# A DeltaNet and feed-forward kernel: the early Gram products, outputs, weight combinations and dummy matmuls are re-ordered

## The chip, the core and the metric

The kernel runs on one core of a Trainium2 chip. The metric is the device time of one execution in microseconds (us). Engines are named as in the profile: PE (TensorE, matmuls), PEld (its weight loads), DVE (VectorE), ACT (ScalarE), POOL (GpSimd) and SP (SyncE, which here only issues DMAs). ACT and POOL issue some DMAs as well.

## What is computed

The first part is a delta-rule attention over 4 batches, 8 heads, 768 steps and a head size of 48. The second is a feed-forward layer over the 3072 rows that come out of it.

```python
k_n = k / (np.linalg.norm(k, axis=-1, keepdims=True) + 1e-06)
for t in range(S):
    y[:, :, t] = np.einsum('bhd,bhde->bhe', q[:, :, t], state)
    v_old = np.einsum('bhde,bhd->bhe', state, kt)
    state = state + bt[:, :, :, None] * np.einsum('bhd,bhe->bhde', kt, vt - v_old)
...
x = y.transpose(0, 2, 1, 3).reshape(B * S, H * D)      # 3072 x 384
h = x @ w_in                                           # 384 x 2048
g = h * (1.0 / (1.0 + np.exp(-1.702 * h)))
return g @ w_out                                       # 2048 x 384
```

The weights arrive as 64-bit floats, so the kernel itself turns the raw words into 32-bit floats.

## The kernel before, in words

**Units.** The 768 steps are cut in 6 chunks of 128. A unit is one chunk of one batch, with all 8 heads; unit n is chunk n // 4 of batch n % 4, and there are 24. A unit needs: its keys scaled to length one; `turn(n)` (line 435), the keys transposed by PE through PSUM into kT; `gram(n)` (412), the product of the keys with themselves per head, copied from two PSUM tiles into G by two copies; `send_blocks` (461), which writes the four 32 x 32 diagonal blocks per head to DRAM (four DMAs, `Nd<-G`); `load_diagonals` (471), which reads them back as one row per block into NT; `invert` (476), which inverts the triangular blocks on DVE (rows `P`, `YB`, `NT`), writes them out (`Yd<-NT`) and reads them back as XB. Then come scores (QS, M), and the solve in four blocks of 32 rows: `solve` (psU) multiplies the inverse with V and ACT copies the result to US, `below` (psR) multiplies it with G, and DVE subtracts that from the rows of V below (`rest`). `outputs` (700) forms psY and the state (psS, added to ST by DVE), ACT copies to xT, and after every second unit six small DMAs move rows of `last` into xT.

**Start.** Chunk 0 (units 0 to 3) has its grams and inversion first. Units 4 to 7 follow: their squares and roots are taken together, and `roots_second` (384) scales the keys of 4 and 5 by 16 ACT copies and those of 6 and 7 by two DVE products. Then the four units of chunk 0 are solved in two pairs. `hops(a, b)` (1090) yields, for a pair, the eight sets of solves and belows, in which one unit's solve shares the set with the other's below; `together` (929) issues a set. Between sets, `fill(us)` (304) issues about so many us of DVE work from a background queue: first the conversion of w_in in nine pieces (`conversions`, 259; each piece is four DVE steps with one ACT Relu and a fifth DVE step), then invert(1) for units 4 to 7, then the conversion of w_out. `feed` (1125) issues six matmuls of the feed-forward layer's first product (`hidden`, 729; PSUM tile ph).

**Steady part.** From line 1170 on, `woven` (975) interleaves the chain of one unit with the matmuls of the feed-forward layer, which `spend` (966) takes from a queue. `normalize` (316) scales the keys of unit m = n + 5 in three stages: POOL squares and DVE sums them; POOL takes the root (`rn`, L325); DVE adds and inverts and POOL multiplies the keys (L329). The rows of the feed-forward layer are multiplied two tiles of 128 at a time with seven half-size products instead of eight (`seven`, 786). For that, `combined` (771) makes T1 to T4 from quarters of w_out in 16 subtractions on POOL (line 762), T1, T2 and T4 into three slots of the buffer TW, T3 in place. TW also holds, at other times, keys of unit 7 and 11 (KX, words 3072 to 3583), the queries, and the GELU results of units 2 and 3.

**Order.** What is called through `vec`, `act`, `pe`, `pool`, `sync` (SP) or `beside` (ACT's DMA queue) is kept in program order on its engine or queue by the helper at line 108, so most rows of the profile name L108, and tiles tell them apart. What is called through `nc.gpsimd` or `nc.sync` directly (normalize, masks and L762 among them) is placed by the compiler's own plan. `warm(n)` (137) issues n dummy bf16 matmuls of 128 x 256 into a PSUM tile that nobody reads.

Of the kernel before, what the change touches and what calls it, by code (L numbers as in the profile page):

```python
# [18 lines left out]
def kernel(  # L19
# [32 lines left out]
    HB = 2  # L52
# [84 lines left out]
    def warm(n, after=None):  # L137
        ps = ps_moe.tile([128, 256], F32, tag="moe", name="ps_warm")
        if after is not None:
            after(ps[:, 0:1], 0.0)  # L140
        for _ in range(n):
            pe.matmul(ps, lhsT=ones[:, 0:128], rhs=ones, start=True, stop=True)
# [66 lines left out]
    def conversion(dst, raw, shape):  # L209

        lo, hi = raw[:, :, :, 0], raw[:, :, :, 1]
        ts, stt = vec.tensor_scalar, vec.scalar_tensor_tensor
        AND, OR = ALU.bitwise_and, ALU.bitwise_or
        E1 = 1 << 20
        p = dst.bitcast(I32)
        ts(p, hi, 0x7FF * E1, None, op0=AND)  # L220
        act.activation(p, p, ACT.Relu, scale=8.0, bias=low)
        yield 0.75
        stt(out=p, in0=hi, scalar=-(1 << 31), in1=p, op0=AND, op1=OR)
        yield 0.95
        ts(hi, hi, E1 - 1, E1, op0=AND, op1=OR)
        yield 0.7
        f = lo.bitcast(F32)
        stt(out=f, in0=lo.bitcast(U32), scalar=2.0**-32, in1=hi, op0=ALU.mult, op1=ALU.add)
        yield 0.95
        stt(out=dst, in0=f, scalar=2.0**-20, in1=dst, op0=ALU.mult, op1=ALU.mult)  # L230
        yield 0.95
# [27 lines left out]
    def conversions():  # L259

        whole = list(pieces())

        def begin(i):
            dst, raw, shape, name = whole[i]
            ops = conversion(dst, places[name[1]] if raw is None else raw, shape)
            return ops, next(ops)

        after, cost = begin(0)
        yield cost
        for i in range(len(whole)):  # L270
            ops = after
            yield next(ops)
            yield next(ops)
            if i + 1 < len(whole):
                after, cost = begin(i + 1)
                yield cost
            yield next(ops)
            cost = next(ops)
            done.add(whole[i][3])
            fetches.pop(whole[i][3], lambda: None)()  # L280
            yield cost
# [31 lines left out]
    def home(n):  # L313
        return KX if n in (len(KN), 3 * B - 1) else KN[n % len(KN)]
# [69 lines left out]
    def roots_second(areas):  # L384

        z, r = (TW[:, a : a + B * H].rearrange("p (b h) -> p b h", b=B) for a in (1792, 1856))
        for o in range(2):
            vec.tensor_reduce(z[:, 2 * o : 2 * o + 2], areas[o], axis=AX.X, op=ALU.add)
        pool.tensor_tensor(r, z, half[:, 0:1].broadcast_to([128, B, H]), op=ALU.pow)
        yield  # L390
        vec.tensor_scalar(r, r, 1e-6, None, op0=ALU.add)
        vec.reciprocal(r, r)
        for o in range(HB):
            K = home(B + o)[:, :, 0:D]
            for h in range(H):
                act.activation(K[:, h], K[:, h], ACT.Copy, scale=r[:, o, h : h + 1])
        yield
        for o in range(HB, B):
            K = home(B + o)[:, :, 0:D]
            vec.tensor_tensor(K, K, r[:, o].broadcast_to([128, H, D]), op=ALU.mult)  # L400
        gate = wk.tile([128, 1], F32, tag="gate", name="gate", bufs=1)
        pool.tensor_copy(gate, KX[:, 0, 0:1])
        yield

    def transposed(src, dst):
        psT = ps_big.tile([128, NP, 128], F32, tag="big", name="psT")
# [5 lines left out]
    def gram(n):  # L412

        c, b = units[n]
        kT = kTs[n]
        G = wk.tile([128, H, 128], F32, tag="G", name="G", bufs=6)
        pool_, tag = (ps_seq, "seq") if c == 0 else (ps_big, "big")
        ps = [pool_.tile([128, NP, 128], F32, tag=tag, name="psG") for _ in range(2)]
        for h in range(H):
            r = slice(h % 2 * 64, h % 2 * 64 + D)  # L420
            pe.matmul(
                ps[h % 2][:, h // 2], lhsT=kT[r, h // 2, :], rhs=kT[r, h // 2, :],
                start=True, stop=True,
            )
        act.activation(G[:, 0::2], ps[0], ACT.Copy)
        if B <= n < 2 * B + HB:
            act.activation(G[:, 1::2], ps[1], ACT.Copy)
        else:
            vec.tensor_copy(G[:, 1::2], ps[1])
        ready[n] = KN[n % len(KN)], kT, G  # L430
        return G

# [43 lines left out]
    def invert(c, b0=0, nb=B):  # L476
# [62 lines left out]
            )  # L539
            yield 0.35 + Q * HS * n / 480  # L540
        if c == 0:
            warm(NY, vec.memset)
        YS = N
        vec.tensor_tensor(YS, Y, bc, op=ALU.mult)
        if c == 0:
# [24 lines left out]
    class Step:  # L570
# [129 lines left out]
        def outputs(self, state=False, between=None):  # L700
            self.turned(
                (0, 4, 1, 5, 2, 6, 3, 7),
                lambda h: self.US[:, h * D : h * D + DP], lambda h: self.M[:, h, :],
                self.c == 0,
            )
            if state:
                self.state(self.psS, between)
            t = slice(self.b % HB * C, (self.b % HB + 1) * C)
            if t.start == 0:
                lasts[0] = wk.tile([128, NTH], F32, tag="last", name="last", bufs=1)  # L710
            last = lasts[0]
            act.copy(last[:, t], self.psY[1][:, 1, :])
            act.copy(self.xT[:, 0::2, t], self.psY[0])
            act.copy(self.xT[:, 1, t], self.psY[1][:, 0, :])

            if t.start > 0:
                t, dma = slice(0, NTH), sync if self.c == 0 else nc.sync.dma_start
                for ct in range(2):
                    for j in range(KC):
                        dma(  # L720
                            out=self.xT[ct * DP + D : (ct + 1) * DP, j, t],
                            in_=last[ct * DP + j * XR : ct * DP + (j + 1) * XR, t],
                        )
# [37 lines left out]
    def add(o, a, b, op, engine=None):  # L761
# [2 lines left out]
    W11, W21 = w_out[:, 0:HF, 0:HM], w_out[:, HF:, 0:HM]  # L764
    W12, W22 = w_out[:, 0:HF, HM:], w_out[:, HF:, HM:]
    T1, T2, T4 = (
        TW[:, i * HF * HM : (i + 1) * HF * HM].rearrange("p (f d) -> p f d", f=HF) for i in range(3)
    )
    T3 = W12

    def combined():

        n = 2
        for o, a, b in ((T1, W12, W11), (T2, W22, T1), (T3, W22, W12), (T4, W21, T2)):
            for f in range(0, HF, n):
                add(o[:, f : f + n], a[:, f : f + n], b[:, f : f + n], sub_)
                yield

    def beside_of(work, other):

        for cost in work:
            next(other, None)
            yield cost
        run(other)

# [118 lines left out]
    def run(work):  # L904
        for _ in work:
            pass
# [38 lines left out]
    def follow(n):  # L945

        if n + 3 < len(units):
            load(n + 3, ((QP, q),))
        m = n - 1 + len(KN)
        if n == B + 1:  # L950
            nc.sync.dma_start(out=KN[m % len(KN)], in_=KX)
        elif n > B and m < len(units):
            load(m, ((KN, k),), nc.gpsimd.dma_start)
        if n - 1 + B < len(units):
            load_values(n - 1 + B)
        if n % HB == 0 and n > B:
            h = (n - 1) // HB
            gT, sums = [], []
            work = hidden(xTs[h], gT, slice(0, NTH), 1.3, sums)
            queue.append(beside_of(work, combined()) if h == HB else work)  # L960
            queue.append(seven(*units[h * HB], gT, sums))
            xTs.pop(h)

    debt = [0.0]

    def spend(cost):

        debt[0] = debt[0] + cost if queue else 0.0
        for done in take(debt[0]):
            debt[0] -= done  # L970
# [4 lines left out]
    def woven(n, share):  # L975
# [24 lines left out]
        ahead_of(inverting, ahead[1])  # L1000
        spend(share / 6)
        next(P, None)
        spend(share / 6)

        together([(B_, 2)], [(D_, 0)])
# [74 lines left out]
        turn(n)  # L1080
    for n in (B, B + 1):
        gram(n)
    run(inverting)
    Ndx = [send_blocks(n) for n in (B, B + 1)]
    run(scaling)
    pool.memset(late_U[:, H * D :], 0.0)
    for s in pair:
        s.select()

    def hops(a, b):  # L1090

# [8 lines left out]
        s.outputs(True, lambda: fill(1.7))  # L1100
        steps.pop(s.n)

    path = hops(*pair[:2])
    for i in range(2 * NB):
        together(*next(path))
        if i in (1, 3):
            turn(B + HB + i // 2)
        if i > 0:
            fill(1.7)
    for n in (B + 2, B + 3):  # L1110
        gram(n)
        Ndx.append(send_blocks(n))
    load_diagonals(Ndx)
    for s in pair[:2]:
        put_out(s)
    sync(out=KN[0], in_=KX)
    load(8, ((KN, k),), sync)
    for f in range(3):
        fetch_out(f)
    for n in range(B, B + 2):  # L1120
        load(n, ((QP, q),), sync)
# [7 lines left out]

    gTs = [], []  # L1130
    ffn.append(hidden(xTs[0], gTs[0], slice(0, NTH), 1.3))
    path = hops(*pair[2:])
    for i in range(2 * NB):
        together(*next(path))
        if i > 2:
            feed()
        fill(1.7)
    for s in pair[2:]:
# [80 lines left out]
```

## Time and profile before

| what | value |
|---|---|
| median of 3 runs | 778.43 us (774.37 to 779.09) |
| profiled execution | 778.5 us, its span 776.8 us |
| PE busy | 730.6 us (94%), 8356 matmuls |
| DVE busy | 487.7 us (63%) |
| ACT busy | 238.6 us (31%) |
| POOL busy | 237.7 us (31%) |
| mean granted PE clock | 0.947 |
| 28 dummies of chunk 0's inversion | 61.37 to 66.79 us |
| first hop of units 0 and 1 | 66.7 us |
| grams of units 6 and 7 on PE | 85.2 to 90.5 us |
| invert(1) starts on DVE | 114.6 us |

A row of a timeline reads: start in us, duration in us, engine, line, operation, out<-in, shapes and count, and in square brackets the idle time of the engine just before and what ended it. A row of the table by stage reads: from and to, then for PE, PEld, DVE, ACT and POOL the busy time and in brackets the number of instructions, then the granted PE clock (1.00 is full, 0.50 is half), the share of the DMA engines and GB/s. A busy PE includes matmuls that are slow for a lower clock.

### The profile page before, as it was taken

The numbers are of one execution on the slowest core, as the hardware profiler recorded it, in microseconds if no ns is written. First come the engines' busy times: TensorE is split into PE (matmuls) and PEld (weight loads), VectorE is DVE, ScalarE is ACT, GpSimd is POOL, SyncE is SP. The second block draws the span as 40 slices with busy tenths as digits, with TensorE's granted clock in tenths as the row PEclk, the third lists the DMA queues.
The fourth block names the chain that finished last, engine by engine and source line by source line (L and its number), as shares of the span: only waits on it lengthen the run. The fifth ranks groups of instructions, "written<-read, shape, count | busy, mean of one in ns | idle before, by whom it ended". The sixth has DMA issues, their size and how long they took to land.

```text
span 776.8 us, 19495 instructions
## 1 busy us (share of the span) xinstructions
PE 730.6 (94%) x8356; PEld 626.8 (81%) x8356; DVE 487.7 (63%) x1013; ACT 238.6 (31%) x527; POOL 237.7 (31%) x210
## 2 busy tenths in 40 slices
PE   8388789989997999999999999999999999999998
PEld 6266668856666898898898898888988988988988
DVE  4796689999768577687687687677677750120000
ACT  3363443533332322422323322322322313222120
POOL 5022001200057362352442542542620611403123
PEclk8576679999999899999999999999999999999999
DMA  9994654531224104104113113113113020000000
GB/s 169 123 173 100 169 127 82 123 102 50 59 46 84 35 13 95 38 19 92 35 25 84 35 27 84 35 31 79 36 23 77 20 56 2 2 27 1 26 1 21
DMA packets 128182, 47.11 MB, mean 61 GB/s; under 512 B 117920, under 2 KB 122144, under 8 KB 128096
## 3 DMA queue, kind: packets, MB, share of 16 engines
q1 hardware_dynamic: 125568, 41.54, 25.7%
q0 software_dynamic: 1344, 3.93, 2.2%
q8 instruction: 66, 1.08, 0.6%
q10 hardware_dynamic: 1184, 0.39, 0.2%
q14 instruction: 20, 0.16, 0.1%
HBM read 33.13 MB, written 11.01 MB: 57 GB/s over the span
## 4 chain that ended last, share of the span: by engine, by line
PE 74%; DVE 15%; DMA 4%; issue 3%; SPq 2%; POOL 2%; ACT 1%; DVEq 0%; POOLq 0%; ACTq 0%
PE ph L108 28%; PE po L108 25%; PE psY L108 5%; PE psU L108 5%; DVE P L108 4%; PE psG L108 4%; PE psQ L108 3%; DVE YB L108 3%; DVE w_out L108 2%; SPq L108 2%; PE psT L108 2%; PE psR L108 2%; DVE NT L108 2%; DMA w_out<-in_moe_w_in_dram 1%; DMA Nd<-G 1%
## 5 line engine op out<-in xcount | busy, mean ns | idle before, releaser
L108 PE MATMUL ph<-xT,w_in 128*128 128x256 f32 x1152 | 266.7, 387 | 0.4 <-DMA xT<-last 0.4
L108 PEld LDWEIGHTS ph<-xT,w_in 128*128 128x128 f32 x1152 | 217.6, 193 | 33.1 <-DVE V L108 1.4
L108 PE MATMUL po<-w_out,gT 128*128 128x192 f32 (+1 forms) x736 | 147.2, 354 | 4.0 <-DVE o L108 3.6
L762 POOL TENSOR_TENSOR gT<-gT 128x512 f32<-128x512 f32 x80 | 105.9, 1332 | 123.9 <-ACT gT L108 113.4
L108 DVE TENSOR_TENSOR V<-V,psR 64x384 f32<-64x384 f32 (+1 forms) x96 | 53.3, 556 | 135.5 <-PE psR L108 134.2
L108 PEld LDWEIGHTS po<-w_out,gT 128*128 128x128 f32 x736 | 121.2, 191 | 19.6 <-DVE o L108 4.6
L108 ACT ACTIVATE gT<-ph 128x512 f32<-128x512 f32 x92 | 54.9, 596 | 147.0 <-PE ph L108 146.9
L108 DVE TENSOR_TENSOR P<-NT,YB 64x2 f32<-64x2 f32 (+9 forms) x200 | 96.0, 480 | 6.2
L108 PEld LDWEIGHTS psU<-V,XB 32*32 32x32 f32 x1536 | 61.3, 109 | 33.6 <-issue 12.8
L108 DVE TENSOR_REDUCE YB<-P 64x2 f32<-64x2 f32 (+9 forms) x200 | 81.8, 409 | 6.9
L108 PE MATMUL po<-TW,gT 128*128 128x192 f32 x480 | 83.0, 328 | 0.0
L108 ACT COPY US<-psU 32x384 f32<-32x384 f32 x92 | 43.2, 469 | 128.5 <-PE psR L108 117.5
L108 PE MATMUL psU<-V,XB 32*32 32x48 f32 x1536 | 72.4, 208 | 9.4 <-DVE V L108 9.2
L108 PEld LDWEIGHTS po<-TW,gT 128*128 128x128 f32 x480 | 77.9, 190 | 1.1 <-issue 0.3
L108 PE MATMUL psR<-US,G 32*32 32x48 f32 x2208 | 63.7, 207 | 4.2 <-ACT US L108 4.1
L108 DVE TENSOR_TENSOR o<-o,po 128x192 f32<-128x192 f32 x40 | 13.5, 351 | 75.8 <-PE po L108 75.3
L108 PEld LDWEIGHTS psR<-US,G 32*32 32x32 f32 x2208 | 54.0, 108 | 5.6 <-ACT US L108 4.9
L631 POOL TENSOR_SCALAR_AFFINE_SELECT M<-M 128x1024 f32<-128x1024 f32 x19 | 22.3, 1173 | 94.3 <-DVE M L108 62.4
L108 DVE TENSOR_TENSOR P<-NT 64x512 f32<-64x512 f32 (+7 forms) x50 | 44.1, 883 | 2.4 <-DVE NT L108 0.5
L108 PE MATMUL psG<-kT 48*128 48x128 f32 x384 | 36.3, 335 | 1.3 <-ACT G L108 1.0
L93 POOL DMA_DIRECT2D KN<-in_k_dram x12 | 11.5, 958 | 84.1 <-PE psY L108 84.1
L108 PE MATMUL psQ<-QS,kT 48*128 48x176 f32 (+1 forms) x368 | 34.5, 330 | 0.8 <-ACT QS L108 0.8
(118 smaller groups left out, 735.7 us busy)
## 6 DMA issues: line engine op xcount, KB each, us to landing
V<-in_v_dram SPq DMA_DIRECT2D x24, 192.0 KB, 3.1
out_dram<-o SPq DMA_DIRECT2D x24, 192.0 KB, 2.1
QP<-in_q_dram SPq DMA_DIRECT2D x22, 192.0 KB, 3.3
raw<-in_moe_w_out_dram SPq DMA_DIRECT2D x9, 384.0 KB, 4.3
NT<-Nd SPq DMA_DIRECT2D x24, 128.0 KB, 2.9
XB<-Yd SPq DMA_DIRECT2D x24, 128.0 KB, 2.9
Nd<-G SPq DMA_DIRECT2D x92, 32.0 KB, 1.8
Yd<-NT SPq DMA_DIRECT2D x22, 128.0 KB, 2.2
```

The costliest lines, as they stand in the source:

```text
L93: dma(out=place(dst, n)[:, :, 0:D], in_=src[b, :, c * C : (c + 1) * C, :].rearrange("h p d -> p h d"),)
L108: return lambda *a, **kw: tc.keep_in_program_order(op(*a, **kw))
L631: (pool if self.n < B else nc.gpsimd).affine_select(out=self.M, in_=self.M, compare_op=ALU.is_gt, fill=0.0, base=0, pattern=[[0, H], [1, 1 ...
L762: (engine or nc.gpsimd).tensor_tensor(o, a, b, op=op)
```

## The change

- `roots_second` scales the keys of all four units by ACT copies, in two stages; the two DVE products and a one-element POOL copy that ordered work behind them are gone. The second stage is issued after the grams of units 4 and 5.
- turn, gram and send_blocks of units 6 and 7, and load_diagonals, are issued before the first set of the first pair, as are fetch_out(0) (one DMA of w_out) and a fill of 4.2. Before, the transposes stood after sets 1 and 3 and the grams after the last set. G of units 0 and 1 lies in tiles of another pool, so that units 2 to 7 have six of their own, and the second copy of gram 6 and 7 goes to DVE.
- After the inversion of chunk 0, 4 dummies instead of 28; after each of the first pair's sets 1 to 6, 4 dummies and a fill of 1.7. No fill after set 7.
- Unit 0's outputs stand in front of the first pair's last set; the first set of the second pair stands before unit 1's outputs. feed begins one set earlier.
- Of the six row DMAs after unit 1, three go by SP and three by ACT's queue.
- A conversion's Relu is issued one step later.
- T1 and T4 exchange their slots in TW. T1's four subtractions are issued in the middle of woven(6), the other twelve beside the last 12 of the 16 steps of the feed-forward product that was beside all of them.

```diff
@@ conversion, conversions
         ts(p, hi, 0x7FF * E1, None, op0=AND)
+        yield 0.75
         act.activation(p, p, ACT.Relu, scale=8.0, bias=low)
-        yield 0.75
+        yield 0.0
...
         after, cost = begin(0)
+        next(after)
         yield cost
...
                 yield cost
+                next(after)
@@ roots_second
-        for o in range(HB):
-            K = home(B + o)[:, :, 0:D]
-            for h in range(H):
-                act.activation(K[:, h], K[:, h], ACT.Copy, scale=r[:, o, h : h + 1])
-        yield
-        for o in range(HB, B):
-            K = home(B + o)[:, :, 0:D]
-            vec.tensor_tensor(K, K, r[:, o].broadcast_to([128, H, D]), op=ALU.mult)
-        gate = wk.tile([128, 1], F32, tag="gate", name="gate", bufs=1)
-        pool.tensor_copy(gate, KX[:, 0, 0:1])
-        yield
+        for os in (range(HB), range(HB, B)):
+            for o in os:
+                K = home(B + o)[:, :, 0:D]
+                for h in range(H):
+                    act.activation(K[:, h], K[:, h], ACT.Copy, scale=r[:, o, h : h + 1])
+            yield
@@ gram
-        G = wk.tile([128, H, 128], F32, tag="G", name="G", bufs=6)
+        G = (
+            g_tile().rearrange("p f (o t) -> p (f o) t", o=2) if n < HB
+            else wk.tile([128, H, 128], F32, tag="G", name="G", bufs=6)
+        )
...
-        if B <= n < 2 * B + HB:
+        if B <= n < B + HB or 2 * B <= n < 2 * B + HB:
             act.activation(G[:, 1::2], ps[1], ACT.Copy)
@@ invert
-            warm(NY, vec.memset)
+            warm(NU, vec.memset)
@@ outputs
-                t, dma = slice(0, NTH), sync if self.c == 0 else nc.sync.dma_start
+                t = slice(0, NTH)
                 for ct in range(2):
+                    dma = (sync, beside)[ct if self.n < HB else 0] if self.c == 0 else nc.sync.dma_start
@@ combined, beside_of, follow, woven
-        TW[:, i * HF * HM : (i + 1) * HF * HM].rearrange("p (f d) -> p f d", f=HF) for i in range(3)
+        TW[:, i * HF * HM : (i + 1) * HF * HM].rearrange("p (f d) -> p f d", f=HF) for i in (2, 1, 0)
...
-        for cost in work:
-            next(other, None)
+        for i, cost in enumerate(work):
+            if i >= FQ:
+                next(other, None)
...
-            queue.append(beside_of(work, combined()) if h == HB else work)
+            queue.append(beside_of(work, combining) if h == HB else work)
...
+    combining = combined()
...
         next(P, None)
+        if n == B + HB:
+            ahead_of(combining, HF // 2)
         spend(share / 6)
@@ the first hops
     for n in (B, B + 1):
         gram(n)
+    next(scaling)
     run(inverting)
     Ndx = [send_blocks(n) for n in (B, B + 1)]
-    run(scaling)
+    for n in (B + 2, B + 3):
+        turn(n)
+    for n in (B + 2, B + 3):
+        gram(n)
+        Ndx.append(send_blocks(n))
...
+    load_diagonals(Ndx)
+    fetch_out(0)
+    fill(4.2)
...
-    path = hops(*pair[:2])
+    path, later = hops(*pair[:2]), hops(*pair[2:])
     for i in range(2 * NB):
         together(*next(path))
-        if i in (1, 3):
-            turn(B + HB + i // 2)
-        if i > 0:
+        if 0 < i < 2 * NB - 1:
+            warm(4)
             fill(1.7)
-    for n in (B + 2, B + 3):
-        gram(n)
-        Ndx.append(send_blocks(n))
-    load_diagonals(Ndx)
-    for s in pair[:2]:
-        put_out(s)
+        if i == 2 * NB - 2:
+            put_out(pair[0])
+    together(*next(later))
+    put_out(pair[1])
...
-    for f in range(3):
+    for f in range(1, 3):
         fetch_out(f)
...
-    path = hops(*pair[2:])
-    for i in range(2 * NB):
-        together(*next(path))
-        if i > 2:
+    for i in range(1, 2 * NB):
+        together(*next(later))
+        if i > 1:
             feed()
         fill(1.7)
```

## The prediction, made before the changed kernel had run

> **What bounds the kernel now.** I read the busy table by stage first, then VectorE's (DVE) timeline, then GpSimd's (POOL) against TensorE's (PE), then the clock. The profiled execution took 778.5 us (span 776.8 and 1.7 around it); the median of the three runs is 778.43, so the sum is made against 778.5 and carries over unchanged.
>
> Busy time by stage (PE, PEld, DVE, ACT, POOL, then granted clock, DMA share, GB/s):
>
> ```profile
> 60.00:80.00 20.00, 15.70 (x318) 12.37 (x318) 13.19 (x21) 6.49 (x11) 4.85 (x7) 0.67 0.57 120
> 80.00:100.00 20.00, 14.59 (x296) 13.12 (x292) 13.74 (x26) 8.73 (x19) 0.00 (x0) 0.67 0.58 150
> 110.00:120.00 10.00, 10.00 (x134) 8.01 (x132) 8.61 (x24) 2.97 (x7) 0.00 (x0) 0.99 0.16 43
> 180.00:200.00 20.00, 19.21 (x233) 12.21 (x233) 18.50 (x52) 7.16 (x18) 1.09 (x1) 1.00 0.11 31
> 200.00:220.00 20.00, 20.00 (x285) 13.56 (x284) 13.64 (x25) 7.09 (x18) 2.16 (x2) 1.00 0.25 58
> 240.00:260.00 20.00, 15.81 (x194) 12.89 (x195) 14.21 (x33) 4.22 (x8) 9.02 (x8) 0.83 0.15 28
> ```
>
> From 110 to 190 DVE is 85 to 95% busy (invert(1), then the weight conversions), and PE has nothing to multiply without converted weights; after 192 PE is full. So what is lost before 114.6, where invert(1) starts on DVE, is lost for good. The second place is 240 to 260, where PE is short by 4.2 us at a lower clock.
>
> DVE between the inversion of chunk 0 and invert(1):
>
> ```profile
> 61.99 0.55 DVE L108 TENSOR_TENSOR TW<-TW 128x384 f32<-128x384 f32 x1
> 69.08 1.14 DVE L108 TENSOR_TENSOR V<-V,psR 32x384 f32<-32x384 f32 x2 [6.54 <-PE psR L108]
> 93.28 0.36 DVE L108 TENSOR_TENSOR ST<-psY,ST 128x192 f32<-128x192 f32 x1 [5.24 <-PE psY L108]
> 97.10 1.14 DVE L108 TENSOR_TENSOR V<-V,psR 32x384 f32<-32x384 f32 x2 [0.72 <-PE psR L108]
> 106.67 0.56 DVE L108 TENSOR_TENSOR V<-V,psR 64x384 f32<-64x384 f32 x1 [1.25 <-PE psR L108]
> 110.71 0.56 DVE L108 TENSOR_TENSOR V<-V,psR 32x384 f32<-32x384 f32 x1 [1.63 <-PE psR L108]
> ```
>
> DVE's holes: 6.54 before the first hop (inverses returning through DRAM), 5.24 while PE does grams 6, 7 and the outputs, then 0.72, 1.25, 1.63. Between 69 and 88 the hops are DVE-bound (0.94 to 1.00 busy in each microsecond), so PE speed is nearly free there.
>
> POOL around 240, and PE at the same place:
>
> ```profile
> 236.84 0.83 POOL L320 TENSOR_TENSOR ksq<-KN 128x384 f32<-128x384 f32 x1 [2.00 <-DMA Nd<-G]
> ...
> 239.54 5.80 POOL L762 TENSOR_TENSOR TW<-w_out,TW 128x384 f32<-128x384 f32 x5
> ...
> 246.35 1.67 POOL L325 TENSOR_TENSOR rn<-ssq,half 128x8 f32<-128x8 f32 x1
> 250.70 1.00 POOL L329 TENSOR_TENSOR KN<-KN,rn 128x384 f32<-128x384 f32 x1 [2.69 <-DVE rn L108]
> ```
>
> ```profile
> 251.76 1.11 PE L108 MATMUL psT<-ident,KN 128*128 128x128 f32 x4 [4.19 <-POOL KN L329]
> ```
>
> Seven weight combinations (0.98 us each) and a mask stand between unit 12's squares and its root; DVE had summed the squares at 238.25. PE waits 4.19 for the scaled keys.
>
> The clock changes only on one grid of 3.41 us. Three of its windows, in which PE was 39, 81 and 22% busy:
>
> ```profile
> 96.60:100.01 3.41, 1.32 (x105) 1.04 (x91) 2.81 (x6) 1.15 (x2) 0.00 (x0) 1.00 0.44 106
> 93.10:96.60 3.50, 2.83 (x94) 2.64 (x94) 3.10 (x7) 2.30 (x7) 0.00 (x0) 0.99 0.43 87
> 246.82:250.23 3.41, 0.75 (x4) 0.32 (x2) 3.04 (x12) 0.60 (x1) 1.19 (x1) 1.00 0.07 10
> ```
>
> At the end of the first and the third it fell to 0.5; after the second it held.
>
> **The change, part by part.** *Grams 6 and 7 first.* Their keys are scaled by ScalarE (ACT): 16 copies that start when gram 5's copy ends (62.15), at the 3.72 us that the other 16 took: 65.87. Behind them on ACT stand two Yd issues (0.84; XB of units 2, 3 land 4 us later, needed only at the second hops), then two kT copies (0.60 each): 67.9. Gram 6 2.6 at half clock, to 70.5; gram 7 can take its PSUM tiles when the first is copied (0.59), 71.1 to 73.4. DVE copies half of each (0.6), the last to 74.1. Then fill(4.2): five conversion steps by their rows (0.61, 0.61, 0.98, 0.98, 0.95) 4.1, to 78.2. The hop's first set (1.4 to 1.5) and its copy behind the third piece's Relu end at 76.8, the second set at 78.2. So DVE's first subtraction comes at 78.3 instead of 69.1: 9.2 later with 4.1 of conversion done, 5.1 behind. DVE's two scalings of keys (1.1) lay in the hole: nothing saved. SP: eight Nd issues (5.6) and four NT (1.8) come forward behind XB; NT lands about 87 instead of 97.7, read at 114; fetch_in(3) leaves 11 us later (85 to 90), read about 100. Cover 5 us; if it fails, each us late is one us of DVE. The 24 dummies dropped ran in the hole, and the POOL gate dropped took 0.18: nothing. fetch_out(0) goes out with them, its slot is free and its reader at 111.9: nothing.
>
> *Middle.* Grams (5.24 of PE, 85.19 to 90.43) are gone from it and unit 0's outputs stand in front of the last set. The sets stay DVE-bound: subtractions 4.6 and three dearer and two cheap fills (6.0 and 2.7) bring the sixth subtraction to 92.2. PE then: dummies to 92.3, outputs and state of unit 0 3.0 (the 1.97 and 1.04 of before), set 7, the first set of unit 2, unit 1's outputs, the next set. In half clock that is 1.5, 1.4, 3.0, 1.5; in full clock 0.9, 0.8, 1.8, 0.9. The subtraction that was at 97.10 falls at 97.6 if all is warm, 102.7 if all is cold, 100.2 if the clock rises after unit 0's outputs, which I take, because it rose at 93.1 after such outputs. The work done by then is equal (ten fills): +3.1.
>
> *Four dummies.* 0.19 each cold (28 took 5.42): 0.77, in the 0.6 to 1.2 in which DVE subtracts; nothing while sets are DVE-bound, and up to 6 x 0.77 = 4.6 if they were not. Do they hold the clock? Set 0.9 and dummies 0.39 in 2.8 us is 46% busy, nearer to the 39% that fell than to the 77 to 81% that held. I take no.
>
> A rule speaks on this. The Trainium skill (TensorE: Matmul & The Clock Gate, "Why this matters for your kernels") says to keep PE's gaps under about 3 us. Here the gap ahead of 100.5 was 1.94 us and the clock fell all the same. By the rule the hops would stay warm without dummies and the middle would be 97.6, some 2.6 us better; by the row it isn't.
>
> *Second hops.* One feed earlier; x rows by two queues, three of six issues (0.4 each) off SP: 1.2 earlier, put on ACT behind unit 2's copy, where the next copy has 1.5 us of slack; if that is gone, 1.2 lost. The holes 1.25 and 1.63 came from feeds at half clock (2.9 instead of 1.3). I take half of them saved; the ends are none and all (2.9). -1.4.
>
> *Relu one step later.* ACT no longer sits on an unfinished first step, but the Relu may stand behind a GELU (0.60). Two steps (1.1 us for 384 wide) lie before the DVE step that needs it: 0, bounds -0.4 and 3 (0.25 x 12 pieces).
>
> So invert(1) starts +3.1 - 1.4 = +1.7, bounds -2.4 (0.5 - 2.9) and +5.6; everything to 192 moves by it.
>
> *Weight combinations.* POOL's unpinned order already takes these as soon as their data allow (the first ran at 223.8, held by PE's last read of its slot in TW). With T1 in the slot behind KX, its four are free after KX's copy at 210 to 212.7; T3 follows PE's reads to about 222. Then some four, not seven, remain at 236.8, or they are spread behind four feeds (4 x 1.3); the key load issued at 232.8 can leave earlier. The root is then done by 240 to 243. But DVE must come there too: its subtraction at 249.62 stands behind ten inversion steps, of which five were slowed beside POOL: 1.96, 0.84, 0.74, 0.74, 0.82 against 1.21, 0.15, 0.17, 0.17, 0.18 elsewhere, 3.2 us. Without these: 246.4, keys scaled 248.5, PE waits 1.0 instead of 4.2: 3.2 saved. The clock window would be 70% busy, near those that held; then the cold 251.8 to 258.9 (transposes 1.11 for 0.44, 18 matmuls 6.0 for 3.89) saves 2.8 more. Bounds: 1.0 (one step fewer) and 7.0 (all). I take 5.5. If T1 were late, four more steps of 0.98 wait, and the first reader is the product after 272.
>
> The Trainium skill (SBUF — State Buffer, "SBUF: two separate sides") calls this an exclusive lock between VectorE and GpSimd. The five slowed rows agree.
>
> Sum: 778.5 + 1.7 - 5.5 = 774.7.
>
> **Rivals.** *A: the hops run warm.* Middle at 97.6, no holes after: -2.4, and all 7.0 at 240: 769.1. For: dummies cut every gap; the grid's phase is free. Against: 46%, and the window of grams alone (58.98 to 62.39) did not raise the clock though PE shows 100% in it. *B, slower than before: POOL's order doesn't clear.* The remaining combinations still stand between squares and root, so 1.0 is saved there, and the front's +1.7 to +3.1 stays: 780. It decides where the root runs after 245. For: the order comes from a plan, not from the chip. Against: T1's slot is free 11 us sooner. *C: the front gives nothing back.* PE cold through the middle and again in the feeds, +5.6, against -5.5: 778.6; with late Relus up to 782. That is also how "no effect" would look.
>
> **How the numbers follow.** Forecast 0.53, A 0.20, B 0.14, C 0.13. "Faster" and "slower" mean by over 1% (7.8 us), about what a measurement of this kernel can tell from no change. Faster needs 770.6: A nearly whole (0.17) and the forecast's low edge (0.06): 0.23. Slower needs 786.2: C with late Relus and grams' SP cover gone: 0.04. Range: low 778.5 - 2.4 - 7.0 and 2.1 for grams at full clock (1.16 for 2.6, part of two): 767; high 778.5 + 5.6 + 1.0 - 1.0 (dummies on the path, POOL's least): 784. The forecast's own range is 770.6 to 778.
>
> **What would show it.** Right: the first subtraction near 78 after a hole of some 9 us; no hole of 5 before the first ST; the subtraction of unit 2 near 100; invert(1) at 114 to 118; the root of unit 12 before 244 and PE's wait for psT under 1.5 with the clock at 1.0. Wrong: a first subtraction before 75; clock 1.0 through the hops; L762 rows still between L320 and L325; DVE holes on w_out after 120 that name ACT.

## The result, and the profile after

| | before | after |
|---|---|---|
| median, same chip, 4 runs each | 777.49 us | 785.06 us |
| profiled execution | 778.5 us | 785.24 us, its span 783.5 us |
| invert(1) starts on DVE | 114.62 | 123.75 |
| mean granted clock | 0.947 | 0.939 |

The changed kernel is slower: ratio 1.0104, 95% interval 1.0062 to 1.0145, where 774.7 us had been forecast. The two profiles show where. Up to the first subtraction of unit 2 the changed kernel is 0.60 behind (97.70 against 97.10), at invert(1) 9.1 behind, at the end 6.7 behind. So some 8.5 us are lost between these two points, and 2.4 come back later.

The busy table by stage of the changed kernel (columns as before); the second row has no counterpart above, so the same ten microseconds of the kernel before stand in the fence after it:

```profile
80.00:100.00 20.00, 16.36 (x339) 13.07 (x338) 16.16 (x29) 7.67 (x18) 0.00 (x0) 0.67 0.37 95
100.00:110.00 10.00, 2.82 (x65) 2.45 (x66) 3.95 (x6) 1.47 (x3) 0.00 (x0) 0.51 0.82 241
110.00:120.00 10.00, 10.00 (x146) 7.40 (x146) 5.25 (x8) 4.01 (x6) 0.00 (x0) 0.64 0.43 104
240.00:260.00 20.00, 17.89 (x183) 14.14 (x180) 15.52 (x38) 7.09 (x16) 14.04 (x12) 1.00 0.39 86
```

```profile
100.00:110.00 10.00, 9.48 (x124) 7.11 (x126) 7.67 (x11) 4.41 (x7) 0.00 (x0) 0.50 0.81 207
```

From 100 to 110 PE falls from 9.48 to 2.82 and DVE from 7.67 to 3.95: both wait for something else. DVE's timeline says for what:

```profile
76.77 1.14 DVE L108 TENSOR_TENSOR V<-V,psR 32x384 f32<-32x384 f32 x2 [0.21 <-PE psR L108]
93.72 0.36 DVE L108 TENSOR_TENSOR ST<-psY,ST 128x192 f32<-128x192 f32 x1 [0.23 <-PE psY L108]
97.70 1.14 DVE L108 TENSOR_TENSOR V<-V,psR 32x384 f32<-32x384 f32 x2 [0.51 <-PE psR L108]
103.93 0.69 DVE L108 TENSOR_SCALAR w_in<-w_out 128x768 int32<-128x768 int32 x1 [4.64 <-DMA w_out<-in_moe_w_in_dram]
113.11 0.56 DVE L108 TENSOR_TENSOR V<-V,psR 64x384 f32<-64x384 f32 x1 [5.13 <-PE psR L108]
```

The 5.24 before the first ST is gone, as the change intends. In its place stand 4.64 for the raw words of w_in's last quarter (fetch_in(3)) and 5.13 behind PE, which itself waits for the feed-forward layer's input. SP's queue (start, length of a run of issues, tiles, count) and, last, ACT's:

```profile
76.27 1.80 SPq L108 DMA_DIRECT2D NT<-Nd  x4
78.58 21.91 SPq L108 DMA_DIRECT2D w_out<-in_moe_w_in_dram  x12
100.79 3.04 SPq L108 DMA_DIRECT2D w_out<-in_moe_w_out_dram  x4
103.92 1.87 SPq L108 DMA_DIRECT2D xT<-last  x3
105.88 0.54 SPq L108 DMA_DIRECT2D KN<-TW  x1
```

```profile
97.63 1.88 ACTq L108 DMA_DIRECT2D xT<-last  x3
```

Twelve issues last 21.91, and everything behind them on SP is late: SP's own x rows at 103.92, KN<-TW at 105.88. The waits of SP's queue between 76 and 112 (total, times, longest) name the cause, and the chain that ended last passes through it:

```profile
SPq L108 <- DMA xT<-last: 11.9, 2, 11.5
```

```profile
98.90 1.80 DMA xT<-last
100.79 0.35 SPq L108
...
105.88 2.79 DMA KN<-TW
108.68 2.92 PE ph L108 x6
```

The profile puts the start of ph down to KN<-TW, SP's next issue behind the x rows. By the compiled program's list of waits the first ph products wait for the x rows, and not for KN<-TW.

SP waits 11.9 for transfers of ACT's queue with which the pieces of w_in have nothing to do. The same list explains it (DMAHW0 to 7 are its names for counters of completions; cut to the rows in question):

```
ACT  xT<-last                (1st, 2nd, 3rd)    waits DMAHW6, DMAHW7, DMAHW0
SP   w_out<-in_moe_w_in      (11th)             waits DMAHW6
SP   w_out<-in_moe_w_in      (12th)             waits DMAHW7
SP   w_out<-in_moe_w_out     (1st)              waits DMAHW0, ...
```

Completions of the DMAs that SP and ACT issue are counted on eight such lanes, handed out in turn in the order of the compiler's plan over both queues. A DMA waits until the one that had its lane before has landed. In the plan ACT's x rows stand ahead of SP's last two pieces; on the chip ACT comes to them at 97.63, long after SP could have sent those pieces.

### The profile page after: what moved, and what is told of

The parts are those of the page before. It is cut to its first block, busy times and chain, and to the rows that moved or that the text cites. A ratio compares the mean times of both kernels' runs of the same rounds, so it can differ in the third digit from the quotient of the medians.

```text
span 783.5 us, 19512 instructions
## 1 busy us (share of the span) xinstructions
PE 735.0 (94%) x8356; PEld 627.8 (80%) x8356; DVE 485.2 (62%) x1013; ACT 241.3 (31%) x541; POOL 238.6 (30%) x209
## 4 chain that ended last, share of the span: by engine, by line
PE 75%; DVE 12%; DMA 4%; issue 3%; POOL 2%; ACT 2%; SPq 2%; ACTq 0%; DVEq 0%; POOLq 0%
PE ph L108 27%; PE po L108 25%; PE psY L108 5%; PE psU L108 5%; PE psQ L108 4%; PE psG L108 4%; DVE w_out L108 3%; PE psT L108 3%; DVE P L108 2%; PE psR L108 2%; DVE YB L108 2%; SPq L108 2%; DMA KN<-in_k_dram 1%; DVE NT L108 1%; POOL TW L764 1%
## 5 line engine op out<-in xcount | busy, mean ns | idle before, releaser
L108 DVE TENSOR_TENSOR P<-NT,YB 64x2 f32<-64x2 f32 (+9 forms) x200 | 92.6, 463 | 6.2
L108 PE MATMUL psR<-US,G 32*32 32x48 f32 x2016 | 56.0, 205 | 6.1 <-ACT US L108 6.1
L108 PEld LDWEIGHTS psR<-US,G 32*32 32x32 f32 x2016 | 47.4, 107 | 7.0 <-ACT US L108 6.7
L108 PEld LDWEIGHTS psG<-kT 48*128 48x128 f32 x384 | 31.5, 231 | 4.6 <-ACT kT L108 1.3
```

Source lines behind the costliest of these rows:

```text
L108: return lambda *a, **kw: tc.keep_in_program_order(op(*a, **kw))
```

## The experiments

Theory 1: the lanes, as told. Rivals: SP is simply full, since 8 Nd and 4 NT issues came forward (theory 2); PE at half clock in the middle (theory 3); a second queue harms by itself (theory 4). "Of before" below means against runs of the kernel before on the same chip.

**All six x rows on SP.** Everything else of the change stays.

```diff
-dma = (sync, beside)[ct if self.n < HB else 0] if self.c == 0 else nc.sync.dma_start
+dma = sync if self.c == 0 else nc.sync.dma_start
```

> The changed kernel with all six x rows issued from SP again; everything else of the change stays. Theory 1 (shared lanes): SP's last fetch_in(3) pieces waited for ACT's x rows, because completions are counted on eight lanes handed out in turn over all queues. Then SP's fetch_in(3) issue is over by about 88 instead of 100.5, VectorE's hole of 4.64 on w_out<-in_moe_w_in_dram goes, the first ph product starts at 101 to 103 instead of 108.7, NT of invert(1) stands at 114 to 117 instead of 123.75, and the time is 776 (774 to 779), about 9 less than the changed kernel. Theory 2 (SP is full: the Nd and NT issues that came forward stand ahead of fetch_in(3)): the hole stays, and the time is 784 to 787. Theory 3 (TensorE at half clock in the middle): the first ph product stays later than 106 with no transfer named before it, and the time is 782 to 786.

Measured: 776.15, ratio of before 0.9994 (0.9965 to 1.0022). SP's queue:

```profile
75.22 9.36 SPq L108 DMA_DIRECT2D w_out<-in_moe_w_in_dram  x12
84.75 1.77 SPq L108 DMA_DIRECT2D w_out<-in_moe_w_out_dram  x4
94.20 4.36 SPq L108 DMA_DIRECT2D xT<-last  x6
```

DVE at the same place:

```profile
94.28 1.14 DVE L108 TENSOR_TENSOR V<-V,psR 32x384 f32<-32x384 f32 x2 [0.51 <-PE psR L108]
95.79 0.69 DVE L108 TENSOR_SCALAR w_in<-w_out 128x768 int32<-128x768 int32 x1
103.08 0.56 DVE L108 TENSOR_TENSOR V<-V,psR 64x384 f32<-64x384 f32 x1 [3.25 <-PE psR L108]
107.22 0.56 DVE L108 TENSOR_TENSOR V<-V,psR 64x384 f32<-64x384 f32 x1 [1.40 <-PE psR L108]
```

Twelve issues in 9.36 with the same Nd and NT ahead of them: theory 2 falls. DVE no longer waits for a transfer there, and the first ph product starts at 98.68. This execution runs some 3.4 ahead of the other from its first 30 us on, so I count from the last row of chunk 0's inversion (`NT<-YB,bI`, at 56.85 here and 60.25 in the changed kernel). Unit 2's first subtraction comes at 37.43 here and 37.45 in the changed kernel, and the clock rises and falls within 0.2 of the same points, so theory 3 falls as the main cause. invert(1) comes at 56.73, against 63.50 in the changed kernel and 54.24 before: all of these 6.8 arise behind unit 2's first subtraction. The two queues alone cost 8.9 by the medians, 8.5 by the ratios.

**Three x rows on POOL's queue.**

```diff
-dma = (sync, beside)[...]
+dma = (sync, other_queue)[...]
```

> The changed kernel with the second queue for the three x rows being POOL's instead of ACT's. Theory 1 (shared lanes): POOL's transfers are counted apart from those that SP and ACT issue, so fetch_in(3) is free of them: the hole of 4.64 goes, time 775 (773 to 779), up to 1.2 less than with all six on SP. Theory 2 (SP is full): 784 to 787. Theory 4 (the second queue itself is the harm, whichever it is, since the x rows land no earlier): 780 or more.

Measured: 778.61, ratio 1.0028 (1.0005 to 1.0050). SP's last piece is out by 87.9 and no DMA hole is left, as theory 1 has it; POOL's DMAs have lanes of their own in the list of waits. The gain over six on SP that I allowed for did not come. In this profile PE's clock rises only at 98.7 (89.8 with six on SP), so the outputs of unit 1 and the set in front of them are at half speed. POOL issues its x rows only at 99.65, too late to have held the clock down there. This execution took 781.38, more than the median; counted as above, its invert(1) comes at 63.20, 6.5 behind six on SP, and 3.9 of that was lost by unit 2's first subtraction, with PE at half clock. So the clock (theory 3) can cost several us in one execution. Whether POOL's issues have a part in the rest was not separated.

**Two queues alone, in the kernel before.**

> The kernel before with the two queues for the x rows alone. Here fetch_in(3) has been issued by 80, some 20 before ACT issues x rows, so if the harm is the place of SP's pieces behind ACT's issue on shared lanes, little is lost here unless another SP transfer shares a lane: within 2 of before. If issuing from ACT is the harm in itself (theory 4): 3 to 9 slower than before.

Measured: 780.47, ratio 1.0049 (1.0026 to 1.0072), so 3.7 slower, more than I expected and in the range that I gave theory 4. Here it is the Nd blocks of units 6 and 7 that got the lanes behind ACT's x rows. Their eight issues before, and now with the two queues:

```profile
88.41 5.87 SPq L108 DMA_DIRECT2D Nd<-G  x8
```

```profile
85.67 13.09 SPq L108 DMA_DIRECT2D Nd<-G  x8
```

SP waits 9.8 for xT<-last there. ACT pays as well: its three issues (1.87) stand in front of the copy of psU, for which PE then waits 2.40. So there are two prices. DVE's hole ahead of unit 2's first subtraction, behind ACT's issues, is 3.22 for 0.72; the one behind the first feed, whose x rows SP issues late, is 3.21 for 1.25. So theory 4 has its part in this kernel. In the changed kernel no such price shows up to unit 2's first subtraction, and behind it DVE's hole for the raw words covers ACT's delay.

**One of the six on ACT.** The sharpest test, since here the lists of waits say that the stall must move to another DMA.

```diff
+other = self.n < HB and ct == 1 and j == 0
+dma = (sync, beside)[other] if self.c == 0 else nc.sync.dma_start
```

> The changed kernel with one of the six x rows on ACT's queue and five on SP. In the list of waits of this kernel ACT's row has lane 6, the last two pieces of fetch_in(3) lanes 4 and 5, and it is the first of the four fetch_outs behind them that waits for lane 6. Theory 1 (shared lanes) therefore has the stall move: the twelve fetch_in(3) issues take about 10, not 21.9, and the hole of 4.64 goes; the fetch_outs leave only when ACT's row has landed, some 6 behind the last fetch_in(3) issue, and the five x rows stand behind them, done 2 to 3 later than with all six on SP. Time 779 (777 to 781). Rival (each issue on ACT harms by its own 0.63): the fetch_outs follow fetch_in(3) at once, and the time is 776.5 to 777.5. Rival (SP is full): the hole of 4.64 stays, 784.

Measured: 780.20, ratio 1.0059 (1.0036 to 1.0082). SP's queue, and ACT's one issue:

```profile
74.93 9.61 SPq L108 DMA_DIRECT2D w_out<-in_moe_w_in_dram  x12
98.10 2.66 SPq L108 DMA_DIRECT2D w_out<-in_moe_w_out_dram  x4
```

```profile
96.22 0.61 ACTq L108 DMA_DIRECT2D xT<-last  x1
```

The twelve take 9.61 and the hole of 4.64 is gone, but SP stands from 84.54 to 98.10, 13.4 of it waiting for that one x row (its longest wait), which ACT issues at 96.22. The five x rows follow, and DVE waits for the products that need them:

```profile
109.43 0.56 DVE L108 TENSOR_TENSOR V<-V,psR 64x384 f32<-64x384 f32 x1 [6.98 <-PE psR L108]
```

So the stall moved to the DMA that the list names, and theory 4 in its simple form (each issue harms by its own length) falls. The sizes were off: the fetch_outs left 13.6 behind the last fetch_in(3) issue, not some 6, and the x rows were all issued 5.0 later than with six on SP (counted as above), not 2 to 3. The time is 4.0 more than with all on SP by the medians, 5.0 by the ratios, but not all of it is the stall's. In the two profiles invert(1) comes 4.6 later; 2.2 of that was lost by unit 2's first subtraction, with unit 1's outputs at half clock, and 2.4 behind it.

**The combining alone, in the kernel before; the front alone.** The first takes only the slots of T1 and T4 and the new places of the subtractions; the second is the change with six rows on SP and without that part.

> The kernel before with one part of the change alone: the slots of the combined weights in the order 2, 1, 0, the combining spread from the fourth step on and drawn ahead at the step of unit 12. The profile of the changed kernel had its late part 3.6 shorter. If this part stands by itself: 3.6 less than before (2 to 5.5), 773 to 776, with TensorE's wait for the scaled keys of unit 12 near 1.9 instead of 4.19. Rival: the late gain came from another part (the clock's grid falling elsewhere): within 1 of before.

> The changed kernel with all six x rows on SP and without the combining part: what is left of the change is the front (grams 6 and 7 ahead of the hops, unit 0's outputs ahead of the last set, dummies, the Relu a step later). If the parts add up: 776.15 + 2.28, the combining's gain by itself, is 778.4 (777 to 780), that is +1.7 to before, the size that the prediction gave the front. Rival: the front is worth nothing by itself, 776.7, and what the combining gives depends on the clock's grid.

Measured: 774.47, ratio 0.9971 (0.9947 to 0.9994), and 780.94, ratio 1.0066 (1.0043 to 1.0089). The parts do not simply add: the combining gives 2.3 by itself, and on top of the front 4.8 by the medians (780.94 to 776.15), 5.6 by the ratios. The time from invert(1) to the end shows why: 662.2 before, 662.9 with the front alone, 660.8 with the combining alone, 658.1 with both. Between the last two, PE comes to unit 12's transposes 1.0 later in the first, and there the clock is at half for one window right behind them (251.6 to 255.0): DVE then waits 3.24 for PE in one and 1.54 in the other, in code that is the same. Thirteen profiles fit this. The four kernels without the combining take 661.7 to 662.9 from invert(1) to the end; of the nine with it, the seven whose clock stays at 1.00 there take 658.0 to 658.3, and the two whose clock falls take 659.8 (the changed kernel) and 660.8. So the gain is 4, or 1.4 to 2.4 where the clock falls there.

**Without the dummies.**

```diff
         if 0 < i < 2 * NB - 1:
-            warm(4)
             fill(1.7)
```

> The changed kernel with all six x rows on SP, and without the four dummies in the six sets of hops. Theory (the prediction's): the dummies neither hold nor lift the clock, so nothing moves: 776 (775 to 777), or 0.4 less, the hole of 0.43 ahead of the sixth subtraction, in which TensorE still runs dummies. Rival: it is the dummies that fill TensorE's windows ahead of unit 0's outputs (four took 1.03 at half clock) and so let the clock rise there; without them unit 0's and unit 1's outputs and the next set run at half clock, 1.7 to 3.3 later: 778 to 779.5.

Measured: 775.57, ratio 1.0006 (0.9985 to 1.0026), the same as with them within 0.3%. In its profile the clock rises 5.4 later, counted as above (at 95.8, against 89.8), but the time does not tell the two apart.

**Dummies where the clock falls.** First behind unit 1's outputs (8) and the next set (16) of the changed kernel with six rows on SP, then 12 in three places, then the same 12 behind the first three sets of units 2 and 3 in the kernel before, with the combining and alone.

> The changed kernel with all six x rows on SP, and with 8 dummies behind unit 1's outputs and 16 behind the next set, where TensorE stood for over 2 us and the clock fell to half. If an idle window is what lets the clock fall: the holes of 3.25 and 1.40 ahead of the next subtractions shrink to 1 or 2 together, 2.5 less: 773.7 (772 to 775.5). Rival: the clock falls for another reason, or the dummies come behind the transfer that they were to bridge: 776 to 777.

> The changed kernel with all six x rows on SP, and with 12 dummies behind each of three places: unit 1's outputs, the next set, and the set in front of the first feed. This is the dummies' pattern that held the clock in the kernel before with the combining part (769.6). If the kernels differ only in how the front is ordered, the holes ahead of the second pair's subtractions go here too: 776.15 less 3 to 5, so 771 to 773. Rival: the front keeps what the dummies give, because TensorE's gap lies ahead of unit 1's outputs or at the first product of the hidden layer, which waits for the x rows: 775 to 776.5, as with 8 and 16.

> The kernel before with the combining part, and with 12 dummies behind each of the first three sets of hops of units 2 and 3. In the profiles of before and of the combining alone the clock fell in the window with 39 per cent of TensorE, and the three feeds at half clock left holes of 1.26, 1.85 and 1.59. If the clock holds: 3 less than 774.5, so 771.5 (770 to 773.5). Rival, as above: 774.5 to 775.5.

> The kernel before with the 12 dummies behind each of the first three sets of units 2 and 3 alone, without the combining. If the two parts add up: 769.6 + 2.3, so 772 (770.5 to 773.5), with TensorE's clock at 1.0 through the three feeds and no holes of 1.26, 1.85, 1.59. Rival: the gain came mostly from the combining, whose late gain is 4 where the clock holds at unit 12 and 1.4 where it falls: 774 to 775.

```diff
         if i > 2:
             feed()
+        else:
+            warm(12)
         fill(1.7)
```

Measured, in this order: 775.45, ratio 1.0000 (0.9979 to 1.0021); 773.71, ratio 0.9954 (0.9932 to 0.9977); **769.59, ratio 0.9915 (0.9895 to 0.9935)**; 773.60, ratio 0.9962 (0.9941 to 0.9982). The third is the fastest kernel here. The dummies alone give 3.1 (773.60, and 776.70 before), which lies between the two times that I had set against each other. By the profiles the rest is the combining's, at its larger size: from invert(1) to the end it is 662.1 without and 658.2 with it. One window of the clock's grid in the combining alone, and the one that answers to it with dummies:

```profile
91.16:94.58 3.42, 2.58 (x102) 2.26 (x98) 2.37 (x5) 2.04 (x6) 0.00 (x0) 1.00 0.65 159
```

```profile
90.98:94.40 3.42, 3.42 (x69) 3.21 (x68) 2.99 (x7) 2.38 (x8) 0.00 (x0) 1.00 0.38 68
```

After the first the clock fell, and the sets and feeds behind it left holes of 1.26, 1.85 and 1.59 on DVE. With dummies it stays at 1.00 until invert(1), and the subtractions follow each other at DVE's pace:

```profile
101.40 0.56 DVE L108 TENSOR_TENSOR V<-V,psR 64x384 f32<-64x384 f32 x1
104.17 0.56 DVE L108 TENSOR_TENSOR V<-V,psR 64x384 f32<-64x384 f32 x1
```

In the front's order the same dummies give less: those behind unit 1's outputs ran at half clock (2.74 for 12) in front of the products that unit 2's subtraction needs, and that hole grew from 0.51 to 3.23, while the 3.25 and 1.40 behind it went. The pattern with 8 and 16 was not taken apart.

**The Relu a step later, on the fastest kernel.**

> The kernel before with the combining part and the 12 dummies behind three sets (769.6), and with the Relu of each conversion one step later, as in the change. The prediction gave this 0 with bounds of -0.4 and 3: 769.6 (769.2 to 772.6). Rival: each later Relu holds VectorE by its distance behind a GELU (0.25 in each of 12 pieces): 772 or more.

Measured: 770.65, ratio 0.9915 (0.9891 to 0.9939): no difference.

## Why the prediction was wrong

**The step that failed** is "x rows by two queues, three of six issues (0.4 each) off SP: 1.2 earlier". I took a second queue for a pure saving of issue time, with ACT's time as its only price. What it left out is that SP's later DMAs wait on lanes that they share with ACT's. SP stood 11.9 for ACT's x rows, the last x row's issue was over at 105.8 instead of 101.2, 4.6 later, and DVE had a hole of 4.64 that the sum did not hold. The two queues cost 8.9 (8.5 by the ratios) where the sum had a gain of 1.2. The 0.4 was off as well: three issues took 1.87. The time, 785.06, lies above the high edge of the range, 784.

**The cover of fetch_in(3).** "Cover 5 us; if it fails, each us late is one us of DVE" had the right place and the right price, and Nd and NT were rightly counted on SP: without ACT's rows the twelve pieces are issued by 84.6, 88.0 in the changed kernel's time. But the text named only what stands ahead on SP as a threat, and left the failure to a chance of 0.04.

**The rule on issuing.** The Trainium skill (Trainium Kernel Development and Optimization, "Key Constraints") says that issuing from several engines saves only the sequencer's issue time. The rows go further: with one issue of 0.61 moved the kernel was 4.0 slower by the medians, of which about half was the stall's in the profiles, and with three 8.9.

**Middle: +3.1.** It was +0.60. Of the 2.5 between, 2.0 had been won by the sixth subtraction (90.22 for the forecast 92.2): the grams in front ended earlier than I summed. Unit 0's outputs at half clock and unit 1's at full were as taken.

**Second hops: -1.4.** Wrong in sign. With six rows on SP the holes are 3.25 and 1.40, 4.65 for 2.88 before; but the combining alone, where this code is untouched, has 4.70. They move by some 2 with the clock, so what the order of the feeds saved, if anything, does not show.

**invert(1): +1.7.** With the queues undone it is +2.5 (56.73 for 54.24), but the combining alone, whose front is that of the kernel before, has 56.47, so one profile cannot tell this from nothing. The whole is 776.15 for the forecast 774.7, within the forecast's own range. The front alone costs 5.1 by its ratio, and 1.7 on top of the combining; that difference was not settled.

**Weight combinations: -5.5.** Right in mechanism, too large in size. Unit 12 after the change, POOL, then DVE, then PE:

```profile
245.65 0.83 POOL L323 TENSOR_TENSOR ksq<-KN 128x384 f32<-128x384 f32 x1 [0.98 <-DMA KN<-in_k_dram]
246.43 4.11 POOL L764 TENSOR_TENSOR TW<-w_out,TW 128x384 f32<-128x384 f32 x4
...
251.55 2.65 POOL L328 TENSOR_TENSOR rn<-ssq,half 128x8 f32<-128x8 f32 x1
258.35 1.00 POOL L332 TENSOR_TENSOR KN<-KN,rn 128x384 f32<-128x384 f32 x1 [4.15 <-DVE rn L108]
```

```profile
250.69 1.98 DVE L108 TENSOR_TENSOR NT<-NT,bI 64x1024 f32<-64x1024 f32 x1 [3.08 <-DMA NT<-Nd]
```

```profile
259.41 0.66 PE L108 MATMUL psT<-ident,KN 128*128 128x128 f32 x4 [1.91 <-POOL KN L332]
```

Four subtractions stand between squares and root, as forecast, instead of seven (that L762 rows stand there at all was also listed as a sign of being wrong, against the sum's own four); PE's wait for psT is 1.91 for 4.19. But what bounds the keys now is DVE. Four of the five slowed inversion steps are fast again (0.16 to 0.19 for 0.74 to 0.84); the first still took 1.98 for 1.96 and, counted from invert(1), starts 0.95 later, when its input has landed. So the transposes come 1.5 earlier, where the sum had 3.2. What the sum put to the clock, 2.8, was some 2.5 with six x rows on SP, where the clock holds at unit 12 (4.1 in all by the profiles), and 0.9 in the changed kernel, where it falls (2.4 in all). The combining alone got 2.3 by its medians, on top of the front 4.8 to 5.6.

**Dummies and Relu: 0.** Both right. Four dummies took 1.03 at half clock, not 0.77.

**Rivals.** A did not happen in the first hops (clock 0.50 from 69 to 93), though the dummies filled PE's windows from 76.28 on to 2.77 of 3.41 and more; its mechanism did pay in the second hops, where the clock had risen already. B did not happen. C's middle did not happen either; the time, 785.06, lies above C's 778.6, and above the 782 with late Relus, for a reason that C does not have.

## What to carry to other kernels

Before a DMA is moved to another engine's queue, look in the program's waits at which later DMAs of the old queue share its completion lane: the late issue of one small transfer holds them all, with all that stands behind them. A queue whose run of issues is far longer than their number times the usual issue, with a tile that it does not use named in its waits, shows this. And dummies paid here where the clock was high and about to fall in front of work that PE bounds, not where it was low.

## What the runs showed that was not expected

- **Lanes across queues.** SP stood 13.4 for a transfer that it neither reads nor issues, after 0.61 of issue had gone to ACT. On POOL's queue the same rows held up no piece of w_in.
- **The share of PE that keeps the clock.** It fell after windows of 3.41 in which PE was busy 1.14 (the changed kernel, 96.76 to 100.17) and 2.58 (the combining alone), and held with 3.42; in the prediction's row it held with 2.83 of 3.50. In and right behind the window of 2.58 PE's gaps were 0.51 and 0.67. The Trainium skill (TensorE: Matmul & The Clock Gate, "Why this matters for your kernels") warns of gaps over about 3 us; here less was enough.
- **What lifts the clock** stays open: from 86.52 to 93.35 PE was busy throughout in the changed kernel and the clock rose, while the window from 76.28 to 79.69, as full, did not raise it; with three rows on POOL it was busy throughout from 86 and the clock stayed at 0.50 until 98.7; with one row on ACT it was busy throughout from 84.65 to 94.89 and the clock stayed at 0.50 until 108.55.
